# Preparing the second layer's weights during the first layer, and a new order of elementwise work in the last rounds

## The chip, the core and the metric

The kernel runs on one core of a Trainium2 chip. A core has TensorE (matrix products, PE in the profile, its weight loads PEld), VectorE (DVE), ScalarE (ACT), GpSimd (POOL) and SyncE (SP), which here only issues DMAs. Each engine works through its own queue in order; they meet at semaphores. The metric is the device time of one execution in microseconds, taken as the median of several runs.

## The reference

A local attention with global tokens (4 batches, 8 heads of 64; 512 local and 32 global positions; window 32) gives 4 x 544 = 2176 tokens of width 512. Two dense layers follow, 512 to 2048 to 512 each:

```
s = where(|i - j| <= 32, q_l k_l^T / 8, -1e9), joined with q_l k_g^T / 8;  out_l = softmax(s) [v_g, v_l]
out_g = softmax(q_g [k_g, k_l]^T / 8) [v_g, v_l];  x = [out_g, out_l] as (2176, 512)
h = x @ w_in;  x = (h * clip(h + 3, 0, 6) / 6) @ w_out            # first layer
h = x @ w_in2; out = where(h > 0, h, exp(min(h, 0)) - 1) @ w_out2  # second layer
```

The layers' weights come as 64-bit floats.

## The kernel before

The 17 tiles of 128 tokens (16 local, one with all global tokens) form five chunks of 4, 3, 3, 3 and 4 tiles (`CHUNKS`). The hidden width is 16 tiles `f` of 128. Every product is made of three: each fp32 operand is split into a high part of reduced precision (`F32R`) and a low rest, and high x high, high x low and low x high are added (`mm3`, L462).

A weight tile of a layer (`load_w`, 1 MB) is converted in stages by `Split`: ScalarE scales the upper word (L123), VectorE shifts (L127), puts in the sign and the low bits (L131, L134), ScalarE makes the high part (L144), VectorE (first layer, L146) or GpSimd (second, L149) the low part. Weight buffers are 16 slots with the tag `w`.

A step is one chunk and one `f`: `up` makes `h` (bank tag `h`, two PSUM banks), then ScalarE, VectorE, ScalarE and VectorE make `g` (L483 to L488), `gh` (L489) and `gl` (L491), and two steps later (`LAG`) `down` multiplies these with the second matrix into up to four banks `acc`. The last `f` of a chunk drains `acc` to `ev` (three buffers, L516, L518), and the first layer stores it to DRAM as `x2d` (L520).

Chunk 0 with its attention and the first layer's conversion is in an order written out by hand (`SCHED`). From chunk 1 on a loop walks the steps; each has three places (`work[0]` to `work[2]`, behind `up`, after each half of `down`) at which other work is issued. `during` spreads the attention of chunk c + 1 over chunk c: for a local tile scores and softmax (`S`, row minima at L282, exponentials at L286), transposes (`T`), values (`O`), transposes back (`XT`) and split (L336, L337). These use two banks with the tag `att`. The second layer's weights are loaded during chunk 4, and `tick` converts them a stage per call, from chunk 4's fifth step through most of the second layer's first part.

The second layer does chunk 1 in the same way ("the standard chunk"). Chunks 2 and 3, and then 0 and 4, are done as pairs by `Super`, with seven products in place of eight on sums of blocks. For that `sform` makes sums of the weight tiles, and stores sums and splits to DRAM (`wd`); `load_stream` reads them back. One round is a pair of chunks and two `f`: seven groups `up` (k = 1, 2, 6, 7, 5, 3, 4) of six products into banks `ua` (tag `h`) and `ub` (`att`), each followed by a group of the round before, `down_b` (a bank `yt`, `att`, which VectorE adds to `y` at L743) or `down_a` (into `acc`). Between them the sums `c11`, `c22`, `c21` and, for four tiles, Relu and Exp on ScalarE (L659, L660), L661 on VectorE, the cast and the subtraction (L665, L666).

SyncE issues all DMAs in program order: the attention's loads, `x2d`, weights, `wd`.

## Time and profile before

| | us |
|---|---|
| median of 3 runs | 910.71 (909.98 to 911.29) |
| the profiled execution | 909.89 |
| its span, first to last instruction | 908.1 |
| busy: TensorE, VectorE, ScalarE, GpSimd | 859.7, 514.2, 422.0, 59.8 |

A busy TensorE here means 95% of the span; the granted clock of TensorE is 0.988 of full speed on average. The rest of the page says in which stretches it is not busy. A row of a time line gives start, duration, engine, line, operation, result and operands; in brackets the idle time before it and what ended it. Products overlap, so a group's length is read from the start of one group to the start of the next.

### The profile page before, as it was taken

The numbers are of one execution on the slowest core, as the hardware profiler recorded it, in microseconds if no ns is written. First come the engines' busy times: TensorE is split into PE (matmuls) and PEld (weight loads), VectorE is DVE, ScalarE is ACT, GpSimd is POOL, SyncE is SP. The second block draws the span as 40 slices with busy tenths as digits, with TensorE's granted clock in tenths as the row PEclk, the third lists the DMA queues.
The fourth block names the chain that finished last, engine by engine and source line by source line (L and its number), as shares of the span: only waits on it lengthen the run. The fifth ranks groups of instructions, "written<-read, shape, count | busy, mean of one in ns | idle before, by whom it ended". The sixth has DMA issues, their size and how long they took to land.

```text
span 908.1 us, 15658 instructions
## 1 busy us (share of the span) xinstructions
PE 859.7 (95%) x6424; PEld 733.2 (81%) x6424; DVE 514.2 (57%) x1043; ACT 422.0 (46%) x795; POOL 59.8 (7%) x40
## 2 busy tenths in 40 slices
...
GB/s 368 419 189 283 83 44 159 76 105 105 147 91 90 105 147 101 70 1 192 172 372 356 350 198 184 304 345 285 178 176 91 139 224 175 131 134 138 22 1 93
DMA packets 38887, 155.34 MB, mean 171 GB/s; under 512 B 3872, under 2 KB 11936, under 8 KB 28576
## 3 DMA queue, kind: packets, MB, share of 16 engines
...
HBM read 122.36 MB, written 31.98 MB: 170 GB/s over the span
## 4 chain that ended last, share of the span: by engine, by line
PE 73%; DVE 13%; ACT 7%; DMA 3%; issue 3%; SPq 1%; DVEq 0%; ACTq 0%
PE acc L462 28%; PE h L462 21%; PE ua L462 8%; PE yt L462 6%; PE ub L462 3%; DMA v<-in_vW 2%; DVE f L131 2%; ACT e L660 2%; PE O L305 1%; DVE e L661 1%; ACT e L659 1%; DMA x2d<-ev 1%; DVE y L743 1%; PE S L273 1%; PE T L87 1%
## 5 line engine op out<-in xcount | busy, mean ns | idle before, releaser
L462 PE MATMUL acc<-gh,w 128*128 128x384 f32 (+1 forms) x640 | 198.2, 365 | 0.0
L462 PE MATMUL h<-x1h,w 128*128 128x384 f32 (+1 forms) x640 | 194.7, 365 | 1.9 <-DVE w L146 1.9
L462 PEld LDWEIGHTS h<-x1h,w 128*128 128x128 f32 x640 | 118.1, 188 | 19.7 <-issue 5.3
L462 PEld LDWEIGHTS acc<-gh,w 128*128 128x128 f32 x640 | 118.7, 188 | 12.7 <-issue 0.6
L484 DVE SCALAR_TENSOR_TENSOR g<-g,h 128x384 f32<-128x384 f32 (+1 forms) x80 | 48.5, 606 | 132.8 <-ACT g L483 132.6
L462 PE MATMUL acc<-gl,w 128*128 128x384 f32 (+1 forms) x320 | 114.9, 359 | 0.8 <-DVE gl L491 0.8
L462 PE MATMUL h<-x1l,w 128*128 128x384 f32 (+1 forms) x320 | 114.9, 359 | 0.2 <-DVE x1l L337 0.2
L489 ACT CAST gh<-g 128x384 fp32r<-128x384 f32 (+1 forms) x96 | 52.8, 550 | 112.5 <-DVE g L484 75.0
L483 ACT ACTIVATE g<-h,half 128x384 f32<-128x384 f32 (+1 forms) x80 | 49.9, 624 | 101.1 <-PE h L462 100.9
L491 DVE TENSOR_TENSOR gl<-g,gh 128x384 fp32r<-128x384 f32 (+1 forms) x96 | 65.7, 685 | 28.2 <-ACT gh L489 28.0
L661 DVE SCALAR_TENSOR_TENSOR e<-e,c 128x384 f32<-128x384 f32 (+1 forms) x48 | 30.0, 626 | 73.8 <-ACT e L660 73.8
L462 PEld LDWEIGHTS acc<-gl,w 128*128 128x128 f32 x320 | 60.2, 188 | 6.5 <-DVE gl L491 1.4
L462 PEld LDWEIGHTS h<-x1l,w 128*128 128x128 f32 x320 | 60.2, 188 | 5.7 <-DVE x1l L337 0.5
L462 PE MATMUL yt<-ga,gg_h 128*128 128x512 f32 x160 | 52.4, 409 | 10.3 <-DVE y L743 9.9
L149 POOL TENSOR_TENSOR w<-f,w 128x512 fp32r<-128x512 f32 x32 | 54.6, 1726 | 81.1 <-ACT w L144 73.3
L462 PE MATMUL h<-x2h,w 128*128 128x384 f32 x128 | 40.6, 382 | 13.8 <-DVE g L488 13.7
L462 PE MATMUL acc<-ga,gg_h 128*128 128x512 f32 x160 | 49.9, 393 | 0.0
L131 DVE SCALAR_TENSOR_TENSOR f<-raw,f 128x1024 int32<-128x1024 int32 (+1 forms) x33 | 45.7, 1385 | 0.2
L462 PEld LDWEIGHTS yt<-ga,gg_h 128*128 128x128 f32 x160 | 29.2, 191 | 20.1 <-DVE y L743 14.8
L462 PE MATMUL ua<-xs,be 128*128 128x384 f32 (+1 forms) x192 | 44.4, 366 | 0.6 <-ACT s L709 0.6
L462 PE MATMUL ua<-xs,al 128*128 128x384 f32 (+1 forms) x192 | 44.5, 367 | 0.0
L462 PE MATMUL ub<-xs,al 128*128 128x384 f32 (+1 forms) x192 | 44.1, 365 | 0.0
...
## 6 DMA issues: line engine op xcount, KB each, us to landing
...
wd<-st SPq DMA_DIRECT2D x16, 512.0 KB, 5.1
wd<-w SPq DMA_DIRECT2D x16, 512.0 KB, 6.4
```

The lines of the kernel that those rows point to most:

```text
L87: nc.tensor.transpose(o, i, ident)
L131: nc.vector.scalar_tensor_tensor(w, self.high[:, s], -0x80000000, w, op0=ALU.bitwise_and, op1=ALU.bitwise_or)
L149: nc.gpsimd.tensor_sub(lo[:, i], self.wf[:, i], hi[:, i].bitcast(F32))
L273: nc.tensor.matmul(self.sp[r][cs, j, :], self.q[rs, j, cs], self.k[rs, j, 32 * i : 32 * i + P], start=True, stop=True,)
L305: nc.tensor.matmul(self.op[r][cs, j, :], self.pt[:, r, j, cs], self.v[:, i, 2 * j + r, :], start=True, stop=True)
L462: nc.tensor.matmul(o, a, b, start=first and i == 0, stop=last and i == len(pairs) - 1, skip_group_check=more)
L483: nc.scalar.activation(g, hp, AF.Relu, scale=1.0 / 6.0, bias=half)
L484: nc.vector.scalar_tensor_tensor(g, g, 1.0, hp, op0=ALU.min, op1=ALU.mult)
L489: nc.scalar.copy(gh, g)
L491: return lambda: nc.vector.tensor_sub(gl, g, gh.bitcast(F32))
L660: nc.scalar.activation(e, e, AF.Exp, scale=-1.0)
L661: nc.vector.scalar_tensor_tensor(e, e, -1.0, h, op0=ALU.add, op1=ALU.max)
```

## The change

- The second layer's weights are no longer loaded whole and converted by `tick`. A generator, `prepare`, is advanced once at each of the three places of every step from chunk 1 on. It loads half tiles (512 KB) into four buffers with the tags `f0` to `f3`, converts them, makes the splits and the four sums, and stores all to DRAM (`wd`, in a new layout). A pair of tiles takes 23 places. The buffers pass from one use to the next, by the roles A, B_, W and X.
- The standard chunk reads its weights back from `wd` (two tiles of 1 MB per pair, `load_stream(-1 - p)`), issued during chunk 4 as weight slots come free. GpSimd no longer subtracts for the weights.
- The sums and operands of the first pair are made one step earlier. The first four value windows use other buffers than the weights' slots.
- In `Super`, two `up` groups stand before the first `down_b`; `yt` alternates between the bank tags `h` and `att`; and the elementwise chain is issued one piece per group: `after(n, ...)` puts a piece at the end of the n-th group from there, the present one counting as the first.

```diff
-                self.w = pool.tile([P, 2, DM], I32, name=f"f{self.m}_{self.f}", tag="f", bufs=3)
+                self.w = pool.tile([P, 2, DM], I32, name=f"f{self.m}_{self.f}", tag=f"f{self.f % 3}", bufs=1)
...
-            if self.m == 0:
-                nc.vector.tensor_sub(lo[:, s], self.wf[:, s], hi[:, s].bitcast(F32))
-                return
-            for i in range(2):
-                nc.gpsimd.tensor_sub(lo[:, i], self.wf[:, i], hi[:, i].bitcast(F32))
...
+    splits = [Split(0, f) for f in range(NF)]
+    wd = [dr.tile([P, 12 * DM], F32, name=f"wd{p}", tag=f"wd{p}") for p in range(NF // 2)]
...
+        def roles(p):
+            return ("f0", "f2", "f1", "f3") if p % 2 == 0 else ("f2", "f0", "f3", "f1")
+
+        def load(p, i, part, tag):
+            raw = pool.tile([P, DM, 2], I32, name=f"raw1_{p}_{i}_{part}", tag=tag, bufs=1)
+            src = w2[2 * p + i].bitcast(I32)[:, part * 2 * DM : (part + 1) * 2 * DM]
+            nc.sync.dma_start(raw.rearrange("p c w -> p (c w)"), src)
+            return raw
...
+        def high(src, n, name, tag):
+            t = pool.tile([P, n, 2, DM // n], F32R, name=name, tag=tag, bufs=1)
+            nc.scalar.copy(t[:, :, 0], src)
+            return t
+        def low(t, src):
+            nc.vector.tensor_sub(t[:, :, 1], src, t[:, :, 0].bitcast(F32))
+        def out(t, p, at):
+            nc.sync.dma_start(wd[p][:, at * DM : at * DM + 2 * DM], t.bitcast(F32).rearrange("p n w k -> p (n w k)"))
+        shaped = lambda w, n: w.bitcast(F32).rearrange("p (n k) -> p n k", n=n)
+        nxt = load(0, 0, 0, "f0"), load(0, 1, 0, "f2")
+        yield
+        yield
+        yield
+        for p in range(NF // 2):
+            A, B_, W, X = roles(p)
+            ra, rb = nxt
+            w = pool.tile([P, 2, DM], I32, name=f"wi{p}", tag=W, bufs=1)
+            wa, wb = w[:, 0], w[:, 1]
+            first(wa, ra)
+            first(wb, rb)
+            yield
+            second(w)
+            third(wa, ra)
+            yield
+            third(wb, rb)
+            ha = high(shaped(wa, 2), 2, f"ha{p}", X)
+            yield
+            low(ha, shaped(wa, 2))
+            hb = high(shaped(wb, 2), 2, f"hb{p}", A)
+            yield
+            out(ha, p, 0)
+            low(hb, shaped(wb, 2))
+            oa = load(p, 0, 1, B_)
+            yield
+            out(hb, p, 2)
+            yield
+            yield
+            sf = pool.tile([P, 4, 2 * P], F32, name=f"sf{p}", tag=X, bufs=1)
+            half = lambda v, k: v.bitcast(F32)[:, 2 * P * k : 2 * P * k + 2 * P]
+            nc.vector.tensor_add(sf[:, 2], half(wb, 0), half(wb, 1))
+            nc.vector.tensor_sub(sf[:, 0], sf[:, 2], half(wa, 0))
+            nc.vector.tensor_sub(sf[:, 1], half(wa, 0), half(wb, 0))
+            nc.vector.tensor_sub(sf[:, 3], half(wa, 1), sf[:, 0])
+            yield
+            s1 = high(sf[:, :2], 2, f"sa{p}", W)
+            yield
+            low(s1, sf[:, :2])
+            s2 = high(sf[:, 2:], 2, f"sb{p}", A)
+            yield
+            out(s1, p, 8)
+            low(s2, sf[:, 2:])
+            yield
+            out(s2, p, 10)
+            w = pool.tile([P, 2, DM], I32, name=f"wo{p}", tag=X, bufs=1)
+            wa, wb = w[:, 0], w[:, 1]
+            first(wa, oa)
+            yield
+            yield
+            ob = load(p, 1, 1, W)
+            second(wa)
+            third(wa, oa)
+            yield
+            yield
+            ha = high(shaped(wa, 1), 1, f"oa{p}", A)
+            yield
+            low(ha, shaped(wa, 1))
+            first(wb, ob)
+            yield
+            out(ha, p, 4)
+            if p + 1 < NF // 2:
+                nxt = (load(p + 1, 0, 0, B_),)
+            second(wb)
+            third(wb, ob)
+            yield
+            hb = high(shaped(wb, 1), 1, f"ob{p}", W)
+            yield
+            low(hb, shaped(wb, 1))
+            yield
+            out(hb, p, 6)
+            if p + 1 < NF // 2:
+                nxt += (load(p + 1, 1, 0, A),)
+            yield
+            yield
...
+            tags = [("p", "pt"), ("xhb", "xlb"), ("vw",), ("qk", "f3")][self.n] if self.early else ("vw",)
+            n, self.v = TPB // len(tags), []
+            for i, tag in enumerate(tags):
+                v = pool.tile([P, n, H, D + 1], F32, name=f"v{self.n}_{i}", tag=tag, bufs=1)
+                nc.sync.dma_start(v, vW[self.b, self.t][:, n * i : n * i + n])
+                self.v += [v[:, j] for j in range(n)]
...
+        def w_in(hl, kd):
+            if m == 0:
+                return wslot[m, f][:, hl, 0, kd * P : kd * P + P]
+            k = kd % 2 * P
+            return sup.stream[-1 - f // 2][0][:, f % 2 * 2 + kd // 2, hl, k : k + P]
...
-                for k in range(max(len(ups), len(downs))):
-                    self.groups += ups[k : k + 1] + downs[k : k + 1]
+                while ups or downs:
+                    n = 2 if len(ups) == len(self.ORDER) else 1
+                    self.groups += ups[:n] + downs[:1]
+                    ups, downs = ups[n:], downs[1:]
 
         def go(self):
             if self.groups:
                 self.groups.pop(0)()
+                now, self.later = self.later, []
+                for wait, what in now:
+                    if wait > 1:
+                        self.later.append((wait - 1, what))
+                    else:
+                        what()
+
+        def after(self, wait, what):
+            self.later.append((wait, what))
...
+            p = self.pairs[g][1] if g >= 0 else -1 - g
+            self.stream[g] = []
+            for i, shape in enumerate(([P, 4, 2, 2 * P], [P, 2, 2, DM], [P, 4, 2, 2 * P])[: 3 if g >= 0 else 2]):
+                t = pool.tile(shape, F32R, name=f"ws{g}_{i}", tag="w", bufs=NF)
+                nc.sync.dma_start(
+                    t.bitcast(F32).rearrange("p i w k -> p (i w k)"), wd[p][:, 4 * i * DM : 4 * (i + 1) * DM]
+                )
+                self.stream[g].append(t)
...
-            if f in (4, 5, 6):
-                now.append(lambda: self.sums(0, f - 3))
-            if 6 <= f < 13:
-                now.append(lambda: self.operand(0, self.ORDER[f - 6]))
+            if f in (3, 4, 5):
+                now.append(lambda: self.sums(0, f - 2))
+            if 5 <= f < 12:
+                now.append(lambda: self.operand(0, self.ORDER[f - 5]))
...
-            nc.vector.scalar_tensor_tensor(e, e, -1.0, h, op0=ALU.add, op1=ALU.max)
-
-            def rest():
-                hi, lo = (self.held[g][w][i] for w in range(2))
-                nc.scalar.copy(hi, e)
-                nc.vector.tensor_sub(lo, e, hi.bitcast(F32))
-
-            self.later.append(rest)
+            self.after(
+                1, lambda: nc.vector.scalar_tensor_tensor(e, e, -1.0, h, op0=ALU.add, op1=ALU.max)
+            )
+            self.after(2, lambda: nc.scalar.copy(hi, e))
+            self.after(3, lambda: nc.vector.tensor_sub(lo, e, hi.bitcast(F32)))
...
+                self.after(1, lambda c=self.c11: self.act(g, 0, c))
...
+                def fourth(b=self.b):
+                    nc.vector.tensor_add(c22, b, s4)
+                    self.after(1, lambda: self.act(g, 3, c22))
+
+                self.after(1, fourth)
-                self.act(g, 3, self.c22)
             elif k == 4:
-                self.later.append(lambda c=self.c21: self.act(g, 2, c))
+                c21 = self.staged(g, "c21", "gl")
+                nc.vector.tensor_add(c21, self.b, self.s2)
+                self.after(1, lambda: self.act(g, 2, c21))
...
-            o, y = bank([P, DM], f"yt{g}_{i}", "att"), self.y[q][:, i]
+            o, y = bank([P, DM], f"yt{g}_{i}", ("h", "att")[i % 2]), self.y[q][:, i]
...
-                v = s - (NC * NF - NF + 4)
-                if v >= 0:
-                    for part in (0, 2) if v % 2 == 0 else (0,):
-                        work[part].append(lambda: tick() if ticks < TICKS else None)
+                for part in range(3):
+                    work[part].append(lambda: next(prep, None))
...
-            if old[:2] == (0, last):
-                load_w(1, old[2])
+            if old[:2] == (0, last) and old[2] % 2:
+                sup.load_stream(-1 - old[2] // 2)
```

VectorE in chunk 1, from the end of tile 7's normalisation (`x7`) to the softmax of tile 8 (the ISA rows; `ev0_0_3` is the last drain of chunk 0, `x1l2` the split of tile 7). Before:

```order
L324 TENSOR_TENSOR x7_1802<-O7_1_1765,sums7_1798 128x4x64
L518 COPY ev0_0_3_1816<-acc0_0_3_748 128x512
L484 SCALAR_TENSOR_TENSOR g0_1_2_1832<-g0_1_2_1832,h0_1_2_1819 128x384
L337 TENSOR_TENSOR x1l2_1844<-XT7_1838,x1h2_1843 128x4x128
L491 TENSOR_TENSOR gl0_1_2_1834<-g0_1_2_1832,gh0_1_2_1833 128x384
L282 ISA P8_1864,mn8_1868<-S8_0_1866,msk_64 128x128
```

Now, from the piece behind `x7` on (`wi0` is the first pair's input half, `ha0` and `hb0` its splits):

```order
L167 TENSOR_SCALAR wi0_1761<-wi0_1761 128x1024
L170 SCALAR_TENSOR_TENSOR wi0_1761<-raw1_0_0_0_1713,wi0_1761 128x512
L173 SCALAR_TENSOR_TENSOR wi0_1761<-raw1_0_0_0_1713,wi0_1761 128x512
L580 COPY ev0_0_3_1832<-acc0_0_3_754 128x512
L170 SCALAR_TENSOR_TENSOR wi0_1761<-raw1_0_1_0_1715,wi0_1761 128x512
L173 SCALAR_TENSOR_TENSOR wi0_1761<-raw1_0_1_0_1715,wi0_1761 128x512
L543 SCALAR_TENSOR_TENSOR g0_1_2_1852<-g0_1_2_1852,h0_1_2_1839 128x384
L391 TENSOR_TENSOR x1l2_1864<-XT7_1858,x1h2_1863 128x4x128
L183 TENSOR_TENSOR ha0_1837<-wi0_1761,ha0_1837 128x2x256
L550 TENSOR_TENSOR gl0_1_2_1854<-g0_1_2_1852,gh0_1_2_1853 128x384
L183 TENSOR_TENSOR hb0_1868<-wi0_1761,hb0_1868 128x2x256
L336 ISA P8_1891,mn8_1895<-S8_0_1893,msk_64 128x128
```

Three pieces of the conversion now stand between `x7` and the drain, two behind it, and two subtractions between `x1l2` and the softmax.

VectorE in the standard chunk, from the activation of its third `f` on (`g1_1_2`; `f1_10` is a weight tile in conversion, `sf4` and `st4` are sums). Before:

```order
L488 SCALAR_TENSOR_TENSOR g1_1_2_5575<-g1_1_2_5575,h1_1_2_5562 128x384
L165 TENSOR_TENSOR sf4_5586<-f1_9_5477 128x256
L166 TENSOR_TENSOR sf4_5586<-sf4_5586,f1_8_5405 128x256
L167 TENSOR_TENSOR sf4_5586<-f1_8_5405,f1_9_5477 128x256
L168 TENSOR_TENSOR sf4_5586<-f1_8_5405,sf4_5586 128x256
L127 TENSOR_SCALAR f1_10_5529<-f1_10_5529 128x1024
L491 TENSOR_TENSOR gl1_1_2_5577<-g1_1_2_5575,gh1_1_2_5576 128x384
L131 SCALAR_TENSOR_TENSOR f1_10_5529<-raw1_10_5316,f1_10_5529 128x1024
L134 SCALAR_TENSOR_TENSOR f1_10_5529<-raw1_10_5316,f1_10_5529 128x1024
L488 SCALAR_TENSOR_TENSOR g1_1_3_5624<-g1_1_3_5624,h1_1_3_5611 128x384
```

Now (`t0_1` and `t0_2` are sums for the first pair's operands):

```order
L547 SCALAR_TENSOR_TENSOR g1_1_2_5865<-g1_1_2_5865,h1_1_2_5852 128x384
L550 TENSOR_TENSOR gl1_1_2_5867<-g1_1_2_5865,gh1_1_2_5866 128x384
L547 SCALAR_TENSOR_TENSOR g1_1_3_5898<-g1_1_3_5898,h1_1_3_5885 128x384
L550 TENSOR_TENSOR gl1_1_3_5900<-g1_1_3_5898,gh1_1_3_5899 128x384
L672 TENSOR_TENSOR t0_1_5912<-raw0_1_5834,raw0_0_5832 128x768
L547 SCALAR_TENSOR_TENSOR g1_1_4_5930<-g1_1_4_5930,h1_1_4_5917 128x384
L550 TENSOR_TENSOR gl1_1_4_5932<-g1_1_4_5930,gh1_1_4_5931 128x384
L674 TENSOR_TENSOR t0_2_5944<-raw0_1_5834,t0_1_5912 128x768
L547 SCALAR_TENSOR_TENSOR g1_1_5_5962<-g1_1_5_5962,h1_1_5_5949 128x384
L550 TENSOR_TENSOR gl1_1_5_5964<-g1_1_5_5962,gh1_1_5_5963 128x384
```

Shifts, bit operations and sums are gone; `g` and `gl` of one `f` stand next to each other, and one operand step comes between.

TensorE at the start of a round of the second pair (`ua11`, `ub11` are groups of round 11, `yt10` of the round before). Before:

```order
L462 MATMUL ua11_7650<-xs1_1_7068,al11_7481 128x512 x6
L462 MATMUL yt10_0_7663<-ga10_7347,gg10_0_7501 128x512 x2
L462 MATMUL yt10_0_7663<-ga10_7347,gg10_2_7503 128x512
L462 MATMUL yt10_0_7663<-ga10_7347,gg10_1_7502 128x512 x2
L462 MATMUL yt10_0_7663<-ga10_7347,gg10_3_7504 128x512
L462 MATMUL ub11_2_7671<-xs1_2_7090,al11_7481 128x512 x6
```

Now:

```order
L516 MATMUL ua11_7830<-xs1_1_7242,ws11_0_7646 128x512 x6
L516 MATMUL ub11_2_7839<-xs1_2_7255,ws11_0_7646 128x512 x6
L516 MATMUL yt10_0_7851<-ws10_1_7510,gg10_0_7681 128x512 x2
L516 MATMUL yt10_0_7851<-ws10_1_7510,gg10_2_7683 128x512
L516 MATMUL yt10_0_7851<-ws10_1_7510,gg10_1_7682 128x512 x2
L516 MATMUL yt10_0_7851<-ws10_1_7510,gg10_3_7684 128x512
```

The first `yt` group moved behind the second product group.

VectorE at the same place (`e10_2` is the last tile's L661 of round 10, `y1` the addition that frees the bank of `yt`). Before:

```order
L661 SCALAR_TENSOR_TENSOR e10_2_7659<-e10_2_7659,c21_10_7624 128x512
L743 TENSOR_TENSOR y1_7366<-yt10_0_7663,y1_7366 128x512
L703 TENSOR_TENSOR c11_11_7678<-ub11_2_7671,s1_11_7657 128x512
L666 TENSOR_TENSOR gg10_3_7504<-e10_2_7659,gg10_1_7502 128x512
L743 TENSOR_TENSOR y1_7366<-yt10_1_7682,y1_7366 128x512
L661 SCALAR_TENSOR_TENSOR e11_0_7698<-e11_0_7698,c11_11_7678 128x512
L743 TENSOR_TENSOR y1_7366<-yt10_2_7702,y1_7366 128x512
```

Now:

```order
L735 SCALAR_TENSOR_TENSOR e10_2_7804<-e10_2_7804,c21_10_7794 128x512
L738 TENSOR_TENSOR gg10_3_7684<-e10_2_7804,gg10_1_7682 128x512
L768 TENSOR_TENSOR c11_11_7846<-ub11_2_7839,s1_11_7837 128x512
L807 TENSOR_TENSOR y1_7554<-yt10_0_7851,y1_7554 128x512
L735 SCALAR_TENSOR_TENSOR e11_0_7848<-e11_0_7848,c11_11_7846 128x512
L807 TENSOR_TENSOR y1_7554<-yt10_1_7869,y1_7554 128x512
L738 TENSOR_TENSOR gg11_l_7829<-e11_0_7848,gg11_h_7828 128x512
```

Before, the first `y1` stood behind the L661 of the round that had just ended; now that is done before the new round begins, and `y1` stands ahead of L661 of `e11_0`.

## Rows read from the trace of the kernel before

**Rows 1.** The core: span from first to last instruction, mean granted clock.
```profile
core 0: 908.1 us, clock 0.988
```

**Rows 2.** Stretches: PE, PEld, DVE, ACT, POOL busy (count), clock, DMA share, GB/s.
```profile
142.00:400.00 258.00, 256.67 (x2813) 235.04 (x2812) 99.74 (x361) 101.03 (x231) 0.00 (x0) 1.00 0.31 102
400.00:487.40 87.40, 87.40 (x387) 72.16 (x386) 65.12 (x72) 41.55 (x55) 28.25 (x16) 1.00 0.66 240
487.40:584.97 97.57, 79.70 (x350) 69.52 (x348) 82.83 (x97) 50.70 (x79) 30.85 (x19) 0.91 0.70 257
```

**Rows 3.** Waits of TensorE in 487.4 to 585: total us, times, longest.
```profile
PE h L462 <- DVE g L488: 13.7, 5, 3.6
PE acc L462 <- ACT ev L516: 3.9, 1, 3.9
```

**Rows 4.** Time line of TensorE, second layer's standard chunk: start, us, line, operands.
```profile
487.40 0.34 PE L462 MATMUL h<-x2h,w 128*128 128x384 f32 x1
...
492.29 0.34 PE L462 MATMUL h<-x2h,w 128*128 128x384 f32 x1
...
575.20 0.34 PE L462 MATMUL h<-x2h,w 128*128 128x384 f32 x1
...
579.40 0.34 PE L462 MATMUL h<-x2h,w 128*128 128x384 f32 x1
...
584.97 1.21 PE L462 MATMUL ua<-xs,al 128*128 128x384 f32 x6
```

**Rows 5.** Time line of VectorE in the standard chunk; idle before in brackets.
```profile
512.78 0.69 DVE L518 COPY ev<-acc 128x512 f32<-128x512 f32 x1 [7.52 <-DMA x2d<-ev]
...
526.01 2.22 DVE L134 SCALAR_TENSOR_TENSOR f<-raw,f 128x1024 int32<-128x1024 int32 x1
...
535.32 1.23 DVE L134 SCALAR_TENSOR_TENSOR f<-raw,f 128x1024 int32<-128x1024 int32 x1
```

**Rows 6.** Time line of TensorE, groups of the seven-product rounds, and the last group.
```profile
689.95 1.21 PE L462 MATMUL ua<-xs,be 128*128 128x384 f32 x6
691.00 0.63 PE L462 MATMUL acc<-ga,gg_h 128*128 128x512 f32 x2
...
692.39 1.23 PE L462 MATMUL ua<-xs,be 128*128 128x384 f32 x6
...
784.83 1.52 PE L462 MATMUL ub<-xs,al 128*128 128x512 f32 x6
786.82 1.65 PE L462 MATMUL yt<-ga,gg 128*128 128x512 f32 x6 [0.46 <-DVE y L743]
...
898.82 5.45 PE acc L462 x24
```

**Rows 7.** Waits of the weight loads of TensorE from 585 on.
```profile
PEld yt L462 <- DVE y L743: 20.0, 19, 3.2
```

**Rows 8.** VectorE's 512-wide conversion pieces, by shape: count, busy us, mean ns.
```profile
L131 DVE SCALAR_TENSOR_TENSOR f<-raw,f 128x512 int32<-128x512 int32 x2 | 1.4, 688 | 0.0
L146 DVE TENSOR_TENSOR w<-f,w 128x512 fp32r<-128x512 f32 x2 | 1.4, 686 | 1.1 <-ACT w L144 1.1
...
L127 DVE TENSOR_SCALAR f<-f 128x512 int32<-128x512 int32 x2 | 0.8, 422 | 2.6 <-ACT f L123 2.6
```

**Rows 9.** An attention tile in chunk 1: time lines of TensorE, then ScalarE.
```profile
153.66 1.14 PE L273 MATMUL S<-qk 64*32 64x128 f32 x62 [0.45 <-DVE x1l L337]
...
159.03 1.03 PE L87 MATMUL T<-ident,P 128*128 128x128 f32 x8
...
155.18 2.45 ACT L286 ACTIVATE P<-P,mn 128x128 f32<-128x128 f32 x8 [2.29 <-DVE mn L282]
```

**Rows 10.** DMA issues (KB each, median us to landing).
```profile
wd<-w SPq DMA_DIRECT2D x16, 512.0 KB, 6.4
...
vN<-in_vN SPq DMA_DIRECT2D x8, 512.0 KB, 3.6
...
x2d<-ev SPq DMA_DIRECT2D x8, 256.0 KB, 4.5
```

130 lines of the change are left out of this document (31 added, 99 removed).

## The prediction, made before the changed kernel ran

> **What bounds the kernel now.** First I read the spans and the stretches of the program [rows 1, 2]. The core's span is 908.1 us and the profiled execution took 909.89, 1.8 more; the median of the three runs is 910.71, 0.8 above it. TensorE runs almost without a gap in the first layer's chunks 1 to 3 (256.67 of 258 us) and in chunk 4 (87.40 of 87.40), all at a granted clock of 1.00. The second layer's standard chunk is different: 79.70 of 97.57 us, clock 0.91, while VectorE is busy for 82.83 and GpSimd for 30.85. So the next view is what TensorE waited for there [rows 3]: 13.7 us for `g` at L488, which VectorE computes, and 3.9 us for the drain copy `ev`. The time line of TensorE [rows 4] tells what this stretch costs undisturbed: near its end the first product of a step comes at 575.20 and 579.40, 4.2 us apart. The first two steps, which still finish the wider chunk 4, take 4.89 (487.40 to 492.29). 14 x 4.2 + 2 x 4.89 + 1.4 for two blocks of 0.7 before the next stage is 70.0 us. It took 97.57: **27.6 us are lost**, and that includes what the slower clock costs, since both sides are wall time.
>
> VectorE's time line shows why [rows 5]. Behind its 7.52 us wait for an `ev` buffer whose store to DRAM had not landed, `g` could not be computed. And it is full of conversion work, whose pieces are slow there: the same 1024-wide L134 takes 1.23 us at 535.32 and 2.22 at 526.01.
>
> The last part, the sixteen rounds of seven-product work, runs from 584.97 to TensorE's end at 898.82 + 5.45 = 904.27: 319.3 us. Undisturbed groups [rows 6] take 1.05 us (six 384-wide products, 689.95 to 691.00), 1.39 (six 512-wide, 691.00 to 692.39). So eight rounds of the first pair are 8 x (7 x 1.05 + 6 x 1.395) = 125.8, eight of the second 8 x 15 x 1.391 = 166.9, and four leftover blocks of the standard chunk 2.8: 295.5. **23.8 us are lost** here. The waits of the weight loads name them [rows 7]: 20.0 us, 19 times, for `y` at L743, the addition that frees the PSUM bank of `yt`. The second round type shows it: the `ub` group starts at 784.83 and should end 1.39 later at 786.2, `yt` starts at 786.82 [rows 6].
>
> **The change, part by part.** *Standard chunk.* Conversion, splitting and sums leave VectorE's queue there (the order shown for this chunk: between two `g` only `gl` and one operand step remain). What stays per step is `g`, `gl` and at most one operand piece; that is the load under which rows 4 show steps of 4.2 us, once the conversions had ended. The `ev` wait stays, but the raw weight loads and the stores of `wd` no longer stand in front of the store it waits for. A 256 KB store landed in 4.5 us at the median [rows 10]. `g` of the next step is needed two steps after it is queued, so 4.5 us hide; I leave 2 us for this boundary. The term is 27.6 - 2 = **-25.6 us** (bounds -16, if the whole 7.5 us wait and 4 more stay, and -27.6).
>
> *Rounds of seven products.* Two things move. `yt` alternates between the tags `h` and `att`, so the bank that a `yt` takes was read four groups earlier, not one product group earlier (TensorE's order of a round shows the new places). And the addition of `y` is queued ahead of the elementwise step that waits for ScalarE's exponential (VectorE's order of a round), where it stood behind it. Both waits of a round (0.6 us each in the second pair) go. What is late next: at the start, two product groups more stand before the first `yt`, but no down block fills the time between the last activation and it; the chain Relu, Exp, L661, cast, subtraction for two tiles on ScalarE ends about 1.1 us late. At the change of pairs, VectorE has twelve pieces 384 wide and three 512 wide, at 0.69 for 512 columns [rows 8] some 8.3 us, and seven operands and a sum 1024 wide, at most 1.38 each, 11.0: up to 19.3 us in a 15.7 us round. That is up to 3.6 us late, of which the wider groups behind it take back a part. I put 6 us for these and what I don't see: 23.8 - 6 = **-18 us** (bounds -6 and -22).
>
> *Chunks 1 to 4.* Per pair of weight tiles VectorE gets shifts of four times 512 columns (0.42 each), eight bit operations and six subtractions (0.69 each) and four 256-wide sums (0.35 to 0.69) [rows 8]: 1.7 + 5.5 + 4.1 + 1.4 to 2.8 = 12.7 to 14.1 us, some 107 in all. A pair is spread over 23 of the 48 parts of a chunk, about 41 us, so VectorE rises from 99.74/258 = 39% to about 70%, and ScalarE, with ten pieces taken at 0.69 as well, from 39% to 55%. For the shapes I take the undisturbed rows, because with GpSimd idle in these chunks [rows 2] I see nothing that stretches them; with the stretched ratio 2.22/1.23 a pair would be 23 us, and VectorE at 95%.
>
> The Trainium skill, "SBUF — State Buffer", section "Who interferes with whom", says that a VectorE instruction with two SBUF inputs and a GpSimd instruction that reads SBUF exclude each other for a whole instruction. Rows 5 agree in kind (2.22 against 1.23 us). By that rule chunks 1 to 3 get the short times, as I took; without it the stretch might belong to VectorE's own load, the 23 us per pair would be the price, and rival (a) below the likelier end.
>
> Does the added work reach TensorE? The product chain has room: `g` is needed two steps (some 10 us) after its product, and in 400 to 487 VectorE, at 65 of 87 us and full at the end, cost TensorE nothing [rows 2]. The attention has less [rows 9]: scores end at 154.80, the exponentials at 157.63, transposes begin at 159.03, a margin of 1.4 us; the next tile's scores already waited 0.45 us for `x1l`. The order shown for chunk 1 tells what is queued before `x1l` and the row minima (the ISA rows) of tile 8: three pieces of the conversion before `ev0_0_3`, two behind it, and two subtractions. The first three fill the time in which VectorE waits for that copy's buffer. The rest delays `x1l` by some 0.45 us and the minima by about 1.1, inside the 1.4. Nine such tiles and eight global tiles go through chunks 1 to 3; most have no conversion piece in front of the minima. I take **+3 us**; bounds 0, and +20 if each of the 17 loses 1.2 us.
>
> The conversion's own stores: `sf` takes the buffer of `ha` three parts (5.4 us) after its store is issued, and VectorE would stand still until it lands. 512 KB landed in 6.4 us in the crowded stretch and in 3.6 us for `vN`, a load in the quiet one [rows 10]; bytes in chunks 1 to 3 go from 102 GB/s to 102 + 5.2 MB per 41 us = 230, below the 257 of the standard chunk [rows 2], so I go by 3.6 and put nothing. At 6.4 it is 1 us per pair, hidden in the slack of the product chain.
>
> *Chunk 0.* The first value windows move to other buffers, which frees weight buffers early and makes the load `qk4` wait until the values of tile 3 are used. The DMA engines have the loads ahead of it to carry until then, so the order of landing changes little. 0, bounds -1.5 and +1.5. Chunk 4: 0.
>
> **Sum.** 909.9 - 25.6 - 18 + 3 = 869.3; with the 0.8 between the profiled execution and the median about **870 us**.
>
> **Rivals.** (a) *Attention pays.* The rise to 70% on VectorE, with ScalarE and VectorE waiting for each other in order, breaks the 1.4 us margins: 17 tiles x 1.2 us = 20 in place of 3, 887 us. For it: the margin, and the 0.45 us wait that exists. Against it: in 400 to 487 VectorE was at 75% and full at times, and TensorE did not notice [rows 2], though no attention ran there. Chance 0.2. (b) *The rounds gain little.* The banks of tag `h` only pass the wait on, or the delayed chain is late for the next `yt`: -6 instead of -18, 882 us. For it: `ua` and `yt` now share a tag. Against it: a bank read four groups, 5 us, earlier. Chance 0.1. (c) *Slower than before.* VectorE's queue stands still behind the stores: `sf` waits for `ha`, and each cast for the store before it, 6 waits per pair. To undo 41 us over the six pairs of chunks 1 to 3 it needs 6.8 us of TensorE per pair beyond a slack of some 5 (estimated: half of the two steps that the chain has): the stores would have to land about 12 us after issue, twice the 6.4 of the crowded stretch. From that point it decides; at 13 us the stretch pays 6 x 8 = 48 and the time is 915. Chance 0.04. (d) The standard chunk stays bound by something hidden under VectorE, such as the `x2d` stores: 10 us more, 880. Chance 0.06.
>
> **How the numbers follow.** The forecast has 0.6, with an own range of 864 to 877. The range of 8 in 10 goes from 862 (all residues nothing: 909.9 - 27.6 - 22 - 1.5 + 0.8 = 860, little of it) to 884, which takes in (b), (d) and the milder half of (a). Rivals (a), (b) and (d) are all faster by far, so faster by over 0.2% (1.8 us, about what a measurement of this kernel can tell from no change) has 0.94, same 0.01, slower 0.05.
>
> **What would show it.** Right: a standard chunk of about 71 us between the first `h` with `x2h` and the first `ua`, at clock 1.00; no `yt` wait for `y` above 1 us but near the change of pairs; chunks 1 to 3 at 258 to 262 us with VectorE at about 180 us busy and bit operations of 0.69. Wrong: `S` or `T` waiting for VectorE by more than 10 us in sum, VectorE idle on stores of `wd`, or `yt` waiting as before.

## The result and the profile after

The changed kernel takes **882.2 us** (median of 4 runs, 879.1 to 883.6) against 910.35 (909.58 to 911.29) for the kernel before on the same chip: a ratio of 0.9686, interval 0.9657 to 0.9714. The forecast was 870, the range 862 to 884. So the sign and the large terms came true, and 12 us of the gain went somewhere else.

The profiled execution took 881.51 us, 28.4 less than before. First the span, then the stretches that answer to [rows 1, 2]; the second layer's standard chunk now runs from 504.80 to 574.02.

```profile
core 0: 879.7 us, clock 0.993
```

```profile
142.00:400.00 258.00, 247.25 (x2699) 223.25 (x2697) 160.12 (x464) 126.28 (x274) 0.00 (x0) 0.99 0.66 220
400.00:504.80 104.80, 103.94 (x511) 87.00 (x511) 58.80 (x101) 41.98 (x74) 3.69 (x2) 1.00 0.69 256
504.80:574.02 69.22, 69.22 (x349) 62.67 (x348) 29.34 (x46) 30.63 (x57) 0.00 (x0) 1.00 0.49 175
```

Read the last row first: TensorE is busy for all of the 69.22 us, at clock 1.00, where it took 97.57 before. The first row shows the bill: 247.25 of 258 us, where it was 256.67, with VectorE at 62%. The time line of TensorE has the two ends of the standard chunk, and in the rounds the two waits that are left near their start and at the change of pairs, then a `yt` of the second pair that follows its `ub` without one:

```profile
504.81 0.34 PE L516 MATMUL h<-x2h,ws-1_0_5286 128*128 128x384 f32 x1
...
574.02 1.23 PE L516 MATMUL ua<-xs,ws 128*128 128x384 f32 x6
...
589.18 0.73 PE L516 MATMUL yt<-ws,gg_h 128*128 128x512 f32 x2 [1.25 <-ACT gg_h L737]
...
703.62 0.79 PE L516 MATMUL yt<-ws,gg_l 128*128 128x512 f32 x1 [3.59 <-DVE gg_l L738]
...
790.07 0.62 PE L516 MATMUL yt<-ws,gg_h 128*128 128x512 f32 x2
```

The waits of the weight loads for `y`, 20.0 us in [rows 7], are gone. The longest waits of TensorE now are these:

```profile
PE S L327 <- DVE x1l L391: 5.3, 6, 2.4
PE yt L516 <- DVE gg_l L738: 3.6, 1, 3.6
PE acc L516 <- DVE ev L580: 2.3, 3, 1.2
```

To see where time comes and goes, I compare when the first product `h` of the same step starts in two traces. This table gives how many us a version is behind the kernel before (negative: ahead), at the third and fifth step of chunk 1 (what the drain of chunk 0 delays lies between), at the start of chunks 2, 3, 4 and of the standard chunk, and at the end of TensorE's work; beside it the length of the standard chunk (97.6 before) and of the rounds (319.3 before). The names are those of the experiments below.

```
version       c1 3rd  c1 5th  c2    c3    c4    std   end    | std    rounds
changed         1.0    7.5    8.7  10.3  15.2  17.4  -28.7   | 69.2   301.5
later           0.6    1.0    2.3   5.4   9.2  10.2  -34.5   | 69.8   302.3
own buffer      0.7    8.5    9.7  15.9  27.0  29.2  -15.8   | 69.2   302.7
yt in att       1.0    6.2    7.5   8.9  14.8  18.0  -25.8   | 69.2   303.9
old rounds      1.4    7.4    8.7   9.4  12.7  15.7  -13.2   | 69.8   318.1
behind          0.5    5.9    9.8  13.7  23.8  28.8  -15.5   | 69.8   302.7
double stores   0.5    1.1    5.2  20.5  33.7  37.4   -7.1   | 70.7   301.6
skip            0.8    1.5    2.2   2.1   3.3  15.6  -25.8   | 74.1   301.4
operands        0.8    1.4    2.8   7.7  11.2  12.3  -38.8   | 69.8   295.9
skip, tails     1.0    1.7    2.6   5.8  12.0  17.8  -23.2   | 74.3   301.5
 + operands     0.8    1.3    1.9   6.8  12.5  18.1  -29.2   | 73.6   295.9
final           1.2    1.8    2.5   2.3   4.4   5.4  -41.4   | 74.1   295.9
```

The changed kernel: 17.4 us late at the standard chunk, of which 6.5 come within two steps at the first chunk boundary; 28.3 won back in the standard chunk, 17.8 in the rounds. Chunk 0 is the same in all versions and ends 0.5 to 1.4 us late in them (first column), which is in every number to its right up to `end`.

### The profile page after: what moved, and what is told of

It reads as the page before. It is cut to its first block, busy times and chain, and to the rows that moved or that the text cites. A ratio compares the mean times of both kernels' runs of the same rounds, so it can differ in the third digit from the quotient of the medians.

```text
span 879.7 us, 15786 instructions
## 1 busy us (share of the span) xinstructions
PE 849.9 (97%) x6424; PEld 731.0 (83%) x6424; DVE 517.6 (59%) x1123; ACT 429.0 (49%) x835; POOL 4.4 (0%) x8
## 4 chain that ended last, share of the span: by engine, by line
PE 74%; DVE 11%; DMA 8%; ACT 5%; issue 2%; SPq 0%; DVEq 0%; ACTq 0%
PE acc L516 26%; PE h L516 19%; PE yt L516 9%; PE ua L516 9%; PE ub L516 6%; DMA raw<-in_w 2%; DMA x2d<-ev 2%; DMA v<-in_vW 2%; DVE g L543 1%; DVE f L131 1%; PE O L359 1%; DVE f L134 1%; DMA wd<-ha 1%; DVE gl L550 1%; PE S L327 1%
## 5 line engine op out<-in xcount | busy, mean ns | idle before, releaser
L516 PEld LDWEIGHTS h<-x1h,w 128*128 128x128 f32 x640 | 119.1, 189 | 20.5 <-issue 5.5
L516 PEld LDWEIGHTS acc<-gh,w 128*128 128x128 f32 x640 | 118.6, 188 | 17.4 <-DVE ev L580 3.4
L516 PE MATMUL ua<-xs,ws 128*128 128x384 f32 (+1 forms) x384 | 88.7, 366 | 0.6 <-ACT s L775 0.6
L516 PEld LDWEIGHTS ua<-xs,ws 128*128 128x128 f32 x384 | 71.1, 189 | 11.5 <-ACT s L775 0.9
L550 DVE TENSOR_TENSOR gl<-g,gh 128x384 fp32r<-128x384 f32 (+1 forms) x96 | 57.4, 599 | 27.1 <-ACT gh L548 25.3
L516 PE MATMUL ub<-xs,ws 128*128 128x384 f32 (+1 forms) x288 | 65.8, 363 | 0.0
L516 PEld LDWEIGHTS ub<-xs,ws 128*128 128x128 f32 x288 | 52.7, 188 | 7.2
L807 DVE TENSOR_TENSOR y<-yt,y 128x512 f32<-128x512 f32 x49 | 33.9, 691 | 39.6 <-PE yt L516 39.0
L732 ACT ACTIVATE e<-c 128x384 f32<-128x384 f32 (+1 forms) x48 | 27.8, 579 | 49.8 <-DVE c L768 16.7
L516 PE MATMUL yt<-ws,gg_h 128*128 128x512 f32 x160 | 50.5, 397 | 1.3 <-ACT gg_h L737 1.3
L516 PE MATMUL acc<-ws,gg_h 128*128 128x512 f32 x160 | 49.9, 393 | 0.0
L735 DVE SCALAR_TENSOR_TENSOR e<-e,c 128x384 f32<-128x384 f32 (+1 forms) x48 | 30.0, 624 | 25.6 <-ACT e L733 25.3
L775 ACT COPY s<-ua 128x384 f32<-128x384 f32 (+1 forms) x16 | 8.5, 533 | 61.0 <-PE ua L516 61.0
```

What stands on the lines that cost most here:

```text
L516: nc.tensor.matmul(o, a, b, start=first and i == 0, stop=last and i == len(pairs) - 1, skip_group_check=more)
L550: return lambda: nc.vector.tensor_sub(gl, g, gh.bitcast(F32))
L732: nc.scalar.activation(e, h, AF.Relu, scale=-1.0)
L735: 1, lambda: nc.vector.scalar_tensor_tensor(e, e, -1.0, h, op0=ALU.add, op1=ALU.max)
L807: nc.vector.tensor_add(y, o, y)
```

## The experiments

Times are medians; each ratio is to the kernel before on the same chip.

### One wait, one shift, and the two halves of the rounds

At the first boundary VectorE copies the fourth drain tile late and everything behind it is late. These are the lines of VectorE before, then of VectorE and of ScalarE in the changed kernel:

```profile
150.70 0.69 DVE L518 COPY ev<-acc 128x512 f32<-128x512 f32 x1 [2.31 <-DMA x2d<-ev]
151.31 0.54 DVE L484 SCALAR_TENSOR_TENSOR g<-g,h 128x384 f32<-128x384 f32 x1
152.92 0.69 DVE L337 TENSOR_TENSOR x1l<-XT,x1h 128x512 fp32r<-128x512 f32 x1 [1.06 <-ACT x1h L336]
```

```profile
154.33 0.69 DVE L580 COPY ev<-acc 128x512 f32<-128x512 f32 x1 [2.98 <-DMA x2d<-ev]
154.94 0.68 DVE L170 SCALAR_TENSOR_TENSOR wi<-raw,wi 128x512 int32<-128x512 int32 x1
155.65 0.69 DVE L173 SCALAR_TENSOR_TENSOR wi<-raw,wi 128x512 int32<-128x512 int32 x1
156.26 0.55 DVE L543 SCALAR_TENSOR_TENSOR g<-g,h 128x384 f32<-128x384 f32 x1
157.87 0.69 DVE L391 TENSOR_TENSOR x1l<-XT,x1h 128x512 fp32r<-128x512 f32 x1 [1.06 <-ACT x1h L390]
```

```profile
148.24 0.67 ACT L164 ACTIVATE wi<-raw 128x512 f32<-128x512 f32 x1 [0.54 <-DMA raw<-in_w]
148.81 0.57 ACT L578 COPY ev<-acc 128x512 f32<-128x512 f32 x1
...
156.84 0.51 ACT L548 CAST gh<-g 128x384 fp32r<-128x384 f32 x1 [2.79 <-DVE g L543]
157.26 0.58 ACT L390 CAST x1h<-XT 128x512 fp32r<-128x512 f32 x1
```

`x1l` is 4.95 us later than before: 3.63 of it is the later copy (0.9 of that was there before the boundary), 1.32 are two conversion pieces behind it. These two cost their full time, although VectorE is idle for 1.06 us ahead of `x1l`: ScalarE's cast `x1h` stands behind `gh`, `gh` waits for VectorE's `g`, and `g` stands behind the pieces, so `x1l` follows `g` by 1.61 us before and after. TensorE waits for the copy itself, which frees a bank of `acc`, and then the scores wait for `x1l`, since it frees the PSUM bank that they take; on TensorE's time line:

```profile
155.08 0.44 PE L516 MATMUL acc<-gh,w 128*128 128x384 f32 x1 [1.17 <-DVE ev L580]
...
158.62 1.74 PE L327 MATMUL S<-qk 64*32 64x128 f32 x55 [2.41 <-DVE x1l L391]
```

My first theory made the copy's wait the cause (a drain buffer whose store to `x2d` had not landed, issued late because ScalarE's drain copy stood behind two activations on a raw weight load). The rival was load: VectorE is fuller, and attention pays wherever it meets a piece.

**Own buffer**: 897.35 us, ratio 0.9846 (0.9826 to 0.9866).

```diff
-        ev = pool.tile([P, n if m == 0 else DM], F32, name=f"ev{m}_{c}_{i}", tag="ev", bufs=3)
+        tag, bufs = (f"xh{'ab'[c % 2]}", 1) if m == 0 and c < 3 and i == 3 else ("ev", 3)
+        ev = pool.tile([P, n if m == 0 else DM], F32, name=f"ev{m}_{c}_{i}", tag=tag, bufs=bufs)
```

> The changed kernel with one edit: the fourth drain copy of chunks 0 to 2 takes a buffer of its own (the finished chunk's xh) in place of the three-buffer ring 'ev', so it waits for no x2d store. Changed kernel: 882.2 us; its chunks 1 to 4 took 16.5 us more than before, of which some 10.8 at the four chunk boundaries, 6.5 at the first. Theory 1 (boundary): VectorE stands at that copy until the first x2d store has landed, and x1l and the next scores stand behind it; then the first three boundaries lose 1 to 2 us each in place of 6.5, 1.6 and 1.5, the half-clock stretch after the first goes too, and the time is 873 to 877. Theory 2 (load): VectorE and ScalarE are simply fuller, and attention pays wherever it meets a conversion piece; then the boundary keeps its jump from the pieces themselves, and the time is 880 to 883.

Neither forecast came true. The fourth copy no longer waits, but the buffer that I took is the one that the next tile's split writes, and ScalarE now stands there for the same store. ScalarE's time line, then TensorE's waits:

```profile
158.61 0.59 ACT L390 CAST x1h<-XT 128x512 fp32r<-128x512 f32 x1 [2.49 <-DMA x2d<-ev]
```

```profile
PE S L327 <- DVE x1l L391: 16.5, 5, 7.2
```

So the run does not decide between the two theories; it shows what a store costs when the bank chain (`XT`, `x1h`, `x1l`, next scores) waits for it: 11.8 us (29.2 against 17.4), nearly all behind the second and third boundary.

**Later**: 876.32 us, ratio 0.9618 (0.9594 to 0.9642).

```diff
-        yield
-        yield
-        yield
+        for _ in range(9):
+            yield
```

> The changed kernel with the whole conversion begun six parts (two steps, about 11 us) later: nine empty places in front of the first pair in place of three. Nothing else moves. Theory 1 (boundary): the pieces of the first pair no longer stand in front of and behind the drain copies of chunk 0, the jump of 6.5 us at the first boundary shrinks to about 1, the other boundaries change by 1 to 2 either way: 875 to 879. Theory 2 (load): the same work meets the same attention tiles two steps later, the jump only moves: 881 to 884.

As the boundary theory said: 0.4 us lost at the first boundary in place of 6.5. The raw loads were still issued ahead of the same boundary, so they are not its cause. What remains, 9.2 us up to the standard chunk, comes mostly at single steps of chunks 1 to 3, where `S` or `SG` waits 0.4 to 1.6 us for `x1l` or `xg`.

**yt in att**: 884.48 us, ratio 0.9706 (0.9684 to 0.9728), and **old rounds**: 897.56 us, ratio 0.9844 (0.9822 to 0.9865).

```diff
-o, y = bank([P, DM], f"yt{g}_{i}", ("h", "att")[i % 2]), self.y[q][:, i]
+o, y = bank([P, DM], f"yt{g}_{i}", "att"), self.y[q][:, i]
```

> The changed kernel with the bank of yt taken from the tag att every time, as before the change; order of the groups and of the elementwise chains as changed. The rounds gained 17.8 us by two moves. If the other bank does most of it, 8 to 14 us come back: 890 to 896, and the weight loads of yt wait for y again. If the earlier place of the addition of y does most of it, 0 to 4 us come back: 882 to 886.

> The conversion moved as in the change, but the seven-product rounds with the groups, the elementwise chains and the bank of yt of the kernel before (only buffer names and the layout of wd as changed). Prices the two halves of the change apart. If the two are independent: 882.2 + 17.8 = 900, with the standard chunk still at 69 us and the weight loads of yt waiting some 20 us for y. If the standard chunk's gain in part only moved into the rounds: the time is nearer 890, since the old rounds then would profit too.

With the old order of groups and chains (the second of the two, for which the methods that the change rewrote were put back) the rounds take 318.1 us and `yt` waits as in [rows 7]; the two halves of the change are independent. With the old bank alone they take 303.9, and one such wait is left:

```profile
PEld yt L516 <- DVE y L800: 20.2, 19, 3.2
```

```profile
PEld yt L516 <- DVE y L807: 1.2, 1, 1.2
```

So the order does it; with the new order in place the second bank is worth 2.4 us at most, and by the intervals of the medians perhaps nothing. The order of the groups and that of the elementwise chains were put back together (with the old bank), and no run has the new bank with the old order, so what each of them would do alone is not shown.

### Order, meeting places, traffic

**Behind**: 895.41 us, ratio 0.983 (0.9806 to 0.9854).

```diff
-                for part in range(3):
-                    work[part].append(lambda: next(prep, None))
...
                 if part < 2:
                     down(*old, part)
+                if cur is not None:
+                    next(prep, None)
```

> The changed kernel with the conversion's pieces at their old parts, but issued behind that part's drain copies and subtraction in place of ahead of them. Only the order in the queues of ScalarE, VectorE and the DMA issues changes. Theory 1 (order at the drain): in the changed kernel the two L164 activations stood ahead of the drain copy ev on ScalarE and its store to x2d was issued 2 us later than before (149.4 against 147.3), and all else waited on that store; behind it, the store goes out as before and the first boundary loses 1 to 3 us in place of 6.5: 876 to 880. Theory 2 (load): the pieces are queued all the same and x1l stands behind them: 881 to 884.

Neither forecast came true: the time is 11 us above the range of the load theory too. My first theory fell here. ScalarE's drain copy is early again and VectorE's copy starts at 151.69, 1.0 us behind the kernel before, and yet the boundary loses 5.4 us. Now all pieces stand between that copy and `g`, of which these are the first and the last:

```profile
146.40 0.59 ACT L578 COPY ev<-acc 128x512 f32<-128x512 f32 x1
```

```profile
152.30 0.68 DVE L167 TENSOR_SCALAR wi<-wi 128x1024 int32<-128x1024 int32 x1
...
155.07 0.69 DVE L173 SCALAR_TENSOR_TENSOR wi<-raw,wi 128x512 int32<-128x512 int32 x1
155.68 0.55 DVE L543 SCALAR_TENSOR_TENSOR g<-g,h 128x384 f32<-128x384 f32 x1
157.29 0.69 DVE L391 TENSOR_TENSOR x1l<-XT,x1h 128x512 fp32r<-128x512 f32 x1 [1.06 <-ACT x1h L390]
```

```profile
158.04 1.29 PE L327 MATMUL S<-qk 64*32 64x128 f32 x48 [4.30 <-DVE x1l L391]
```

`x1l` again follows `g` by 1.61 us. What counts here is less when the copy's buffer comes free than what is queued ahead of `g`, and so of `x1l`. Behind this boundary the version loses another 23 us up to the standard chunk, the changed kernel 10; TensorE there mostly waits 1 to 3 us at a time for `xg`, `x1l`, the copy `ev` and ScalarE's `PT`. These places were not taken apart.

**Skip**: 884.66 us, ratio 0.9706 (0.9681 to 0.9731). `frees` holds the last stage of each attention tile, the one that frees the bank.

```diff
-                    work[part].append(lambda: next(prep, None))
+                    i = 3 * f + part
+                    near = m == 0 and (i in (2, 3, 4) or (c < last and any(st in frees for st in during(c, i + 1))))
+                    for _ in range(0 if near else 2 if (m, c) == (0, last) and i % 2 else 1):
+                        work[part].append(lambda: next(prep, None))
```

> The changed kernel, in which no conversion piece is issued in the parts that hold the drain copies of a finished chunk (parts 2 to 4) nor in the part just before a local tile's split (x1l) or a global tile's values (xg), whose VectorE result frees the bank that the next scores take; what falls behind is caught up by two pieces in every second part of chunk 4. If the losses of chunks 1 to 3 are these two meeting places (bank chain and drain), nearly all 16.5 us come back but some 3: 868 to 872. If any VectorE and ScalarE load in order costs, wherever it stands, the same work in fewer parts costs as much: 879 to 884. A third way: chunk 4 is overfull with two pieces in a part and the products pay there, 872 to 878 with waits for g in chunk 4.

Up to chunk 4 this is the first outcome: chunks 1 to 3 lose 2.5 us (0.8 to 3.3) where the changed kernel loses 14.2, with five of the eight weight pairs still converted beside attention (six in the changed kernel) and VectorE busy for 154.62 us from 142 to 400, in place of 160.12. So load as such costs little; the places cost. Then chunk 4 pays 12.3, and the time of 884.66 lies above all three ranges. There three pieces of the conversion go into two parts in place of two, and ScalarE stands in front of raw weights that have not landed, with `g` queued behind; the lines of ScalarE, then of TensorE:

```profile
482.95 0.66 ACT L164 ACTIVATE wi<-raw 128x512 f32<-128x512 f32 x1 [6.67 <-DMA raw<-in_w]
```

```profile
489.19 0.80 PE L516 MATMUL h<-x1h,w 128*128 128x512 f32 x1 [5.20 <-DVE g L543]
```

The last pieces still fall into the standard chunk, which takes 4.9 us more than in the changed kernel.

**Double stores** (made on *later*): 900.14 us, ratio 0.9864 (0.9833 to 0.9895).

```diff
+    wx = [dr.tile([P, 12 * DM], F32, name=f"wx{p}", tag=f"wx{p}") for p in range(NF // 2)]
...
-            nc.sync.dma_start(wd[p][:, at * DM : at * DM + 2 * DM], t.bitcast(F32).rearrange("p n w k -> p (n w k)"))
+            for d in (wd, wx):
+                nc.sync.dma_start(d[p][:, at * DM : at * DM + 2 * DM], t.bitcast(F32).rearrange("p n w k -> p (n w k)"))
```

> The version begun six parts later (876.3 us) with each store of a converted piece made twice, the second to a DRAM buffer that nothing reads: 24 MB more traffic, no work more on the other engines. Theory of order (queues of ScalarE and VectorE): the time stays within 2 us, 875 to 878. Theory of traffic (x2d stores and loads land late because the DMA engines carry the conversion): what is left of the extra in chunks 1 to 4, some 9 us, doubles: 882 to 888, and x2d<-ev and qk land later.

A miss for the theory of order alone: 24 us more than *later*, with no compute work more; only SyncE issues 48 further stores. The theory of traffic is right in sign and 12 us short; at the median `qk` lands in 6.1 us (5.7 in *later*), the larger `x2d` stores in 4.7 (3.9), the raw loads of 512 KB in 6.4 (5.4). Chunk 2 shows the loss, 5.2 to 20.5. The way from the stores to TensorE is again a queue: ScalarE stands in front of raw loads that have not landed (19.9 us, 6.4 in *later*) and of buffers whose stores have not landed, the exponentials and activations stand behind, and TensorE waits: 7.3 us for transposes, and 13.9 for `x1l` and `xg` ahead of scores. ScalarE's waits, then TensorE's:

```profile
ACT wi L165 <- DMA raw<-in_w: 19.9, 6, 6.6
ACT oa L180 <- DMA wx<-sb: 10.7, 3, 6.5
ACT wo L165 <- DMA raw<-in_w: 10.7, 4, 3.2
ACT sb L180 <- DMA wx<-hb: 8.0, 6, 4.2
```

```profile
PE T L87 <- ACT P L341: 7.3, 3, 3.4
```

So there are two mechanisms: pieces that stand ahead of an instruction that frees a bank, and pieces that make their engine wait for a DMA. Whether the DMAs are late here through the traffic or through SyncE's longer queue is open. The changed kernel has the second mechanism too: 2.5 of the 14.2 us fall at the first step of chunk 3, where ScalarE waits 3.91 us for a raw load and the transposes behind it 1.39.

**Operands** (made on *later*): 872.35 us, ratio 0.9566 (0.9543 to 0.9588).

```diff
-                self.operand(q + 1, k)
+                self.after(6, lambda: self.operand(q + 1, k))
...
-                nc.vector.tensor_sub(self.t[q, 2], raw(0, 1), self.t[q, 2])
-                self.t[q, 4] = self.t[q, 2]
+                t = self.t[q, 2] if q == 0 else pool.tile([P, 2, self.n(q)], F32, name=f"t{q}_4", tag="p", bufs=1)
+                nc.vector.tensor_sub(t, raw(0, 1), self.t[q, 2])
+                self.t[q, 4] = t
...
+            if p == NF // 2 - 2 and q + 1 < len(SUPER) and k == 4:
+                self.sums(q + 1, 4)
...
-                    n = 2 if len(ups) == len(self.ORDER) else 1
+                    n = (3 if g == 1 else 2) if len(ups) == len(self.ORDER) else 1
```

> The version begun six parts later (876.3 us) with three edits in the rounds: the operands of the second pair are issued six groups later, so they lie half in the round behind the change of pairs; their fourth sum is made one round earlier into a buffer of its own; the first round with down blocks has three product groups ahead of its first yt, in place of two. At the change of pairs yt waited 3.6 us for gg_l, and the clock lost 1.8 more; at the start it waited 1.25 and ua 0.57. Theory (VectorE's queue too full for one round): 6 us come back, 869 to 872. Rival (the wait is the chain of Relu, Exp, cast and subtraction itself, whatever else is queued): at most 1.5 us for the start, 874 to 876. If the later operands are late themselves: slower than 877, with ua or ub waiting for xs.

The rounds are 6.4 us shorter, as the theory said; the median, 872.35, is 4 us below *later* and just above the range of 869 to 872. (The chunks before them, the same code as in *later*, came 2.1 us later in this profile: so far apart are two profiles of one order, and smaller differences in the table say little.) The stretch around the change of pairs, in the changed kernel and here (columns as in [rows 2]):

```profile
700.00:720.00 20.00, 16.41 (x66) 13.39 (x66) 11.21 (x18) 10.03 (x17) 0.00 (x0) 0.91 0.24 95
```

```profile
700.00:720.00 20.00, 20.00 (x89) 16.35 (x88) 13.07 (x21) 10.66 (x19) 0.00 (x0) 1.00 0.66 250
```

VectorE's queue was too full for one round, as the prediction had worked out: the wait of 3.59 us and the slower clock behind it are gone. The third edit gained nothing: `ua` waited 1.52 us for `s` in place of `yt` 1.25 for `gg_h`, and without it (in *+ operands* below) the rounds take 295.9 us as well.

### Putting it together

**Skip, tails**: 886.34 us, ratio 0.9737 (0.9719 to 0.9755), and the same **+ operands**: 880.96, ratio 0.9676 (0.9654 to 0.9698). The edit against *skip*:

```diff
-                    for _ in range(0 if near else 2 if (m, c) == (0, last) and i % 2 else 1):
+                    more = m == 0 and (i >= 44 if c < last else i % 6 == 5)
+                    for _ in range(0 if near else 2 if more else 1):
```

> The version that skips the meeting places, with the catching up moved out of chunk 4: two pieces in the last four parts of chunks 1 to 3, where no attention stage is left, and in every sixth part of chunk 4 alone; the conversion ends some ten parts later than in the changed kernel. With the pieces two to a part all through chunk 4 the start of the standard chunk came 16 us late against the kernel before, 3.2 of it from chunks 1 to 3 and 12.5 from chunk 4, where ScalarE stood up to 6.7 us in front of raw loads. Theory (meeting places, and spacing of the pieces against their DMAs): chunks 1 to 3 still lose 3 to 4, chunk 4 1 to 2: 868 to 872. Rival (the load has to be paid somewhere): the loss only moves again, 878 to 884.

> The run beside it with two of the edits in the rounds: the operands of the second pair six groups later, and their fourth sum a round earlier in a buffer of its own (the third edit, three product groups ahead of the first yt, is left out, since ua then waited 1.52 us for s). At the change of pairs these took away the 3.6 us wait and the slow clock behind it. If the two places are independent: 4 to 5 us below the run beside it, 864 to 868. If not, above 868.

Both forecasts for *skip, tails* failed, the rival's 878 to 884 too. Four parts with two places each cost 3.3 us at the first step of chunk 2, 5.5 at the first two of chunk 3 and 3.4 at the second and third of chunk 4. At the first of these places ScalarE waits for a store and then for a raw load, the exponentials come late, and the transposes wait. ScalarE, then TensorE:

```profile
230.24 0.62 ACT L179 CAST oa<-wo 128x512 fp32r<-128x512 f32 x1 [2.30 <-DMA wd<-sb]
232.58 0.66 ACT L164 ACTIVATE wo<-raw 128x512 f32<-128x512 f32 x1 [1.72 <-DMA raw<-in_w]
...
234.75 2.44 ACT L340 ACTIVATE P<-P,mn 128x128 f32<-128x128 f32 x8
```

```profile
235.28 2.29 PE L87 MATMUL T<-ident,P 128*128 128x128 f32 x8 [2.15 <-ACT P L340]
```

That is the second mechanism alone, with the first one out of the way. The operands are worth 5.4 us here, where 4 to 5 were forecast for two independent places (880.96 itself is far above the 864 to 868 that went with it), and 4 by the medians on *later*; so the places add up.

**Final**: **867.04 us**, ratio 0.953 (0.9517 to 0.9543), the fastest version, with the operands later: skipping, never two places of the conversion in a part, the conversion left to run into the standard chunk. `ready` holds the pairs whose last store has been issued.

```diff
-                    work[part].append(lambda: next(prep, None))
+                    i = 3 * f + part
+                    near = m == 0 and (i in (3, 4) or (c < last and i == 2) or (c < last and any(st in frees for st in during(c, i + 1))))
+                    if not near:
+                        work[part].append(lambda: next(prep, None))
...
-                sup.load_stream(-1 - old[2] // 2)
+                due.append(old[2] // 2)
+            while due and due[0] in ready:
+                sup.load_stream(-1 - due.pop(0))
```

> The meeting places skipped (no piece in parts 2 to 4 of chunks 1 to 3 and 3 to 4 of chunk 4, none ahead of a bank-freeing x1l or xg), never two pieces in a part, and the conversion left to end in part 24 of the standard chunk; the last pair's weights are loaded when its pieces are stored. With the two edits for the change of pairs. Theory 1 (two mechanisms: pieces ahead of bank-freeing work, and ScalarE standing in front of a raw load or a store when pieces follow closer than their DMAs land): chunks 1 to 3 lose 3 as in the first skipping version, chunk 4 1, the standard chunk 0 to 3 since VectorE has 22 us of pieces in 32 us there, rounds as in the run before: 864 to 870. Theory 2 (the load has to be paid somewhere): the standard chunk pays what chunks 1 to 4 gain, 872 to 878.

```profile
142.00:400.00 258.00, 254.65 (x2796) 231.21 (x2795) 153.50 (x457) 125.28 (x276) 0.00 (x0) 1.00 0.60 200
```

```profile
152.48 0.69 DVE L583 COPY ev<-acc 128x512 f32<-128x512 f32 x1 [2.98 <-DMA x2d<-ev]
```

It is 5.4 us late at the standard chunk, 3.2 lost in chunks 1 to 3 and 1.0 in chunk 4. VectorE's fourth drain copy at the first boundary still waits 2.98 us for its buffer, as in the changed kernel, and the boundary loses 0.6 us in place of 6.5. That answers my first theory once more: the wait costs little when no piece stands around it. The standard chunk pays 4.9 us against the changed kernel for the conversion's end, more than the 0 to 3 of the forecast and less than the skipping gains. It is the second mechanism again: a cast on ScalarE waits for a store, `g` is late behind it, and TensorE waits 2.12 us and, two steps later, 1.36:

```profile
518.06 0.62 ACT L181 CAST sb<-sf 128x512 fp32r<-128x512 f32 x1 [4.84 <-DMA wd<-hb]
```

## Why the prediction was right, and where it was not

**Standard chunk**, -25.6: measured 97.57 - 69.22 = 28.3. The 2 us left for its boundary were not needed, and a step takes 4.15 us there, not the 4.2 read from [rows 4], so it is 0.7 beyond the bound of -27.6. The cause is as predicted in kind: VectorE is busy for 29.34 us there, before for 82.83, and TensorE waits for no `g`. *Old rounds* has about the same standard chunk (69.8 us), so the gain does not come from the rounds' half of the change. The work left VectorE and GpSimd at once, and no run parts these two.

**Rounds**, -18: measured 319.3 - 301.5 = 17.8, with the two residues where they were put: 1.25 and 0.57 us at the start (1.1 forecast), 3.59 at the change of pairs (up to 3.6), then a slower clock, 0.91. Of the two moves that were named, the other bank carries next to nothing once the new order is there; the order, of groups and chains together, carries the rest.

**Chunks 1 to 4**, +3: this is the term that failed; it is 16.4 (17.4 at the standard chunk less 1.0 at chunk 1's third step). The step was the sentence that three pieces "fill the time in which VectorE waits for that copy's buffer", so that the rest delays `x1l` by some 0.45 us. It took the copy's wait as fixed, and looked at VectorE alone. `x1l` came 4.95 us late: ScalarE's queue had changed too, so the `x2d` stores that the copies wait for were issued at 149.41 in place of 146.55; and the two pieces behind the copy cost 1.32 us and not 0.45, since what looked like idle time ahead of `x1l` was the way of `g` through ScalarE. *Behind* showed that undoing the first half does not help, since then all pieces come after the wait. The bound of +20 held, and the standard chunk gave 2.7 us more than forecast; so the time lies in the range, 1.8 us from its end. Of the signs that were to show the prediction right, the one for chunks 1 to 3 (258 to 262 us) failed: the same steps took 272.5.

Rival (a), with 0.2, had the right engine chain and the wrong shape: not 17 tiles of 1.2 us each, but a few places. *Later* has the same pieces in the same number of parts and is 7 us earlier at the standard chunk, and *skip* loses 2.5 us in all three chunks.

**Stores of the conversion**, nothing: VectorE's wait for `ha` was small, 2.3 us once, as worked out; but the same question was not asked of ScalarE. `wd<-hb` landed in 7.1 us at the median, not the 3.6 that I went by (the other five stores of a pair in 2.9 to 4.0), and raw loads made ScalarE wait. The waits of VectorE, of ScalarE, and the DMA's row in the changed kernel:

```profile
DVE sf L219 <- DMA wd<-ha: 2.3, 1, 2.3
```

```profile
ACT wi L164 <- DMA raw<-in_w: 9.5, 5, 3.9
```

```profile
wd<-hb SPq DMA_DIRECT2D x8, 512.0 KB, 7.1
```

*Double stores* shows how near this is to deciding: rival (c) looked for the standing queue on VectorE above all; it is ScalarE's that stands, and with twice the stores the version takes 24 us more.

**VectorE's load**, 180 of 258 us forecast, is 160.12 in that window and 169.36 for the same steps, which now take 272.5 us; its pieces have the undisturbed price beside attention:

```profile
142.90:415.40 272.50, 261.75 (x2813) 237.50 (x2813) 169.36 (x487) 132.64 (x290) 0.00 (x0) 0.99 0.65 215
```

```profile
L170 DVE SCALAR_TENSOR_TENSOR wi<-raw,wi 128x512 int32<-128x512 int32 x12 | 8.3, 688 | 0.2
...
L167 DVE TENSOR_SCALAR wo<-wo 128x512 int32<-128x512 int32 x11 | 4.6, 421 | 0.5 <-ACT wo L164 0.5
```

That agrees with the rule of the Trainium skill, "SBUF — State Buffer", section "Who interferes with whom", that was weighed: with GpSimd idle the pieces are not stretched, with VectorE at 62%. No run put GpSimd's work beside them.

**Chunk 0**, 0: +1.0 in this profile, inside its bound. **Chunk 4**, 0: +2.2, of which 1.4 fall into its first steps, with the drain. **The sum**: 28.3 + 17.8 - 17.4 = 28.7 against 28.4 measured.
